# Attention with two MoE layers on one core: MoE 2 with its weight blocks outermost and converted in place, and 32x32 triangles inverted on 128 partitions

## The chip, the cores and the metric

One core of a Trainium2 chip runs the whole program. The metric is the device time of one execution, in microseconds (us); the kernel before takes 1393.04 us, the median of three runs (1391.51 to 1396.16).

## What is computed

A linear attention with a decaying state (4 batches, 8 heads, 768 steps, head size 40), then two feed-forward layers on its 3072 tokens of 320 values. MoE is the reference's own word for them; there is no routing.

```python
for t in range(S):
    y[:, :, t] = einsum('bhd,bhde->bhe', rt, state)
    Sa = einsum('bhde,bhe->bhd', state, at)
    state = state * wt[:, :, None, :] - einsum('bhd,bhe->bhde', Sa, bt) + einsum('bhd,bhe->bhde', vt, kt)
# moe 1: d_ff = 2048
h = x @ w_in
x = (h * clip(h + 3, 0, 6) / 6) @ w_out
# moe 2: d_ff = 1536
out = ((x @ w_a) * (x @ w_b)) @ w_out
```

All inputs but the five weight matrices are float32. The weights are float64, and the kernel turns their two 32-bit words into a float32 with one ScalarE and five VectorE instructions (`f32_steps`, L71 to L86). Every matmul of the two layers then runs on a high and a low float32r part (`split`, L128 to L130).

## The kernel before

The steps are cut into 12 chunks of 64 (`NCH`), each with 16 pairs of heads (`NP`) side by side. `window(j)` (L696) lists by hand the steps of chunk j together with those that prepare chunks j+1 and j+2; all five engines and the DMA queue of SP take their instructions in that order. Between these steps the table `MOE` puts in the steps of the first layer, 16 to a window from window 2 on, where a step is one `up` (16 matmuls) or one `down` (12 matmuls). One window is a period of the attention phase.

**The triangle.** Each chunk needs the inverse of unit triangular 64x64 matrices. Their two 32x32 diagonal blocks, 64 of them in all, go through DRAM (`t_load`, tensor `scr`) into `TA2` with one block to a partition. `t_solve` (L505 to L518) inverts them on POOL: 31 times a product (L515) and a subtraction (L518) over the part of the block that is left, on 64 partitions. Chunks take the lower and the upper 64 partitions in turn. `t_store` (L521 to L539), one window later, turns the result on ScalarE into `tnt` (L528, which uses the free rows of `TA2`), writes it both ways to DRAM (`n1`, `n2`, shown in the profile as `n`) and loads from there `NY` and `AB`; the first matmuls that read it are those of `merge_y` (L547).

**The weights of layer 2.** `WEIGHT` slots of the windows run `widen` (L744): in 68 pieces of 192 columns it loads float64 words (`ws`), converts them (`cv`), and stores float32 to DRAM (`w2af`, `w2bf`, `w2of`). A window has seven slots. After the last window come the 21 steps of layer 1 that are left, below called the tail of layer 1; beside them `moe2_weights` loads the float32 weights back and splits them, one piece after each step from the third on, in turn on POOL and VectorE.

**Layer 2.** `moe2`: for each of six groups of 512 tokens, for each of 12 blocks of 128 inner units, `up` (L842: 16 matmuls of 512 columns) and `down` (L864 to L866: 12 matmuls of 320 columns) into four accumulators that live through all 12 blocks; then the sums go to DRAM.

```python
ac.activation(out=g, in_=uf, func=AF.Relu, bias=bias3, scale=1.0)          # L313, in layer 1's up
g = wk1.tile([128, 512], F32, tag="g", name="g", bufs=1)
for f in window(j): ...   elif f == WEIGHT: next(wide2, None); next(wide2, None)
```

Of the kernel before, what the change touches and what calls it, by code (L numbers as in the profile page):

```python
# [23 lines left out]
NT = B * S  # L24
# [70 lines left out]
def attention_and_moe(ctx, tc, t, flag):  # L95
# [22 lines left out]
    w1 = m1.enter_context(tc.tile_pool(name="w1", bufs=1))  # L118
# [243 lines left out]
    TN2 = a1.tile([128, 32, 32], F32, name="TN2")  # L362
# [15 lines left out]
    def setup_first():  # L378
# [12 lines left out]
        gp.memset(TN2, 0.0)  # L391
# [5 lines left out]
        for z in n2:  # L397
            sp.dma_start(out=z.rearrange("a p s t -> (a p) s t")[:, :, 0:32], in_=TN2[0:32])

# [92 lines left out]
    def t_half(j):  # L492
        return slice(64 * (j % 2), 64 * (j % 2) + 64)

    def t_load(j, between=lambda: None):
# [8 lines left out]
        sp.dma_start(out=TA2[t_half(j)], in_=scr.rearrange("u a p s t -> (u a p) s t"))  # L504

    def t_solve(rws, eng):

        TA, TN, TT = TA2[rws], TN2[rws], TT2[rws]
        nr = rws.stop - rws.start
        eng.memset(TN, 0.0)  # L510
        eng.memset(TN.rearrange("q s t -> q (s t)")[:, 0:1024:33], 1.0)
        for u in range(31, 0, -1):
            n = 32 - u
            tv = TT[:, 0:u * n].rearrange("q (s t) -> q s t", s=u)
            eng.tensor_tensor(  # L515
                out=tv, in0=TA[:, 0:u, u:u + 1].to_broadcast([nr, u, n]),
                in1=TN[:, u:u + 1, u:32].to_broadcast([nr, u, n]), op=ALU.mult)
            eng.tensor_tensor(out=TN[:, 0:u, u:32], in0=TN[:, 0:u, u:32], in1=tv, op=ALU.subtract)  # L518

    def t_start(j):  # L520
        t_solve(t_half(j), gp)  # L521

    def t_store(j, between=lambda: None):
        TN = TN2[t_half(j)]
        r0 = t_half(j).start
        tnt = TA2[r0:r0 + 32]
        NY = py["NY"] = a2.tile([128, NP, 32], F32, tag="py", name="NY")
        ac.copy(out=tnt, in_=TN[0:32].rearrange("q s t -> q t s"))  # L528
        n1 = dram.tile([2, 2, NP, 32, 32], F32, tag="n1", name="n1", bufs=2)
        z, AB = n2[j % 2], ABs[j % 2]  # L530
        sp.dma_start(out=n1[0].rearrange("a p s t -> (a p) s t"), in_=TN[0:32])
        sp.dma_start(out=z.rearrange("a p s t -> (a p) s t")[:, :, 32:64], in_=TN[32:64])
        sp.dma_start(out=n1[1].rearrange("a p s t -> (a p) s t"), in_=tnt)
        between()
        for ab in range(2):
            r = 64 * ab
            sp.dma_start(out=NY[r:r + 32], in_=n1[1, ab].rearrange("p s t -> s p t"))
            sp.dma_start(out=AB[r + 32:r + 64], in_=z[ab].rearrange("p s t -> s p t"))
            sp.dma_start(out=AB[r:r + 32, :, 0:32], in_=n1[0, ab].rearrange("p s t -> s p t"))  # L539

    def merge_y(j):
        AB, NY = ABs[j % 2], py["NY"]
        ps = bank().rearrange("q (p c) -> q p c", p=NP)
        for p in range(NP):
            for ab in range(2):
                r = 64 * ab
                mm(ps[r + 32:r + 64, p], AB[r:r + 32, p, 32:64], NY[r:r + 32, p], start=True, stop=True)  # L547
# [192 lines left out]
    WC = (("w2a", 3 * FF2), ("w2b", 3 * FF2), ("w2o", 12 * DM))  # L740
    w2f = {n: (dram.tile([128, c], F32, name=n + "f") if wide else t[n].rearrange("q k c -> q (k c)")) for n, c in WC}

    def widen():
        pieces = [(t[n].rearrange("q k c -> q (k c)")[:, c0:c0 + 192], w2f[n][:, c0:c0 + 192])  # L744
                  for n, cols in WC for c0 in range(0, cols if wide else 0, 192)]
        loaded, made = [], None
        for i in range(len(pieces) + 3):
            if made:
                sp.dma_start(out=made[0], in_=made[1])
                made = None  # L750
            if i < len(pieces):
                loaded.append((pieces[i][1], words(pieces[i][0], sp)))
            yield
            if loaded and (i > 1 or i >= len(pieces)):
                dst, st = loaded.pop(0)
                made = dst, from_words(st)
            yield

    def moe2_weights(pool):
        r = {}  # L760
# [458 lines left out]
```

## Time and profile before

| | |
|---|---|
| median of 3 runs | 1393.04 us |
| the profiled execution | 1393.52 us |
| its span in the profile | 1391.7 us |
| setup and windows 0 and 1 | 0 to 253 us |
| windows 2 to 9 | 253 to 828 us, 69.7 to 73.2 us each |
| windows 10 and 11 | 828 to 888 and 888 to 926 us |
| tail of layer 1 | 926 to 978 us |
| layer 2 | 978 to 1392 us |
| TensorE / VectorE / ScalarE / GpSimd busy | 82% / 60% / 37% / 38% |

The windows are told apart by ScalarE's copy L528, which begins once in each. PE is TensorE's matmul, DVE is VectorE, ACT is ScalarE, POOL is GpSimd, SP the engine whose queue issues the DMAs. PEclk is TensorE's granted clock as a share of 2.4 GHz.

### The profile page before, as it was taken

The page shows a single profiled execution, that of the slowest core. Times are in us where ns is not written, and L with a number is a line of the kernel's source. Part 1 is how long each engine was busy: PE and PEld are TensorE (multiplying, and loading weights), DVE is VectorE, ACT ScalarE, POOL GpSimd, SP SyncE. Part 2 cuts the span into 40 slices and gives each one's busy share as a digit, 9 for nine tenths or more (in the row PEclk, how much of TensorE's full clock was granted, in tenths as well). Part 3 has the DMA queues.
Part 4 walks back from the last instruction along what each step waited for, and adds up shares of the span by engine and source line. Part 5 has one row for each costly group of instructions (what it writes and reads, how often), then busy time and mean ns, then how long its engine had stood idle before and what let it go on. Part 6 is the DMA issues. An engine that isn't in the chain of part 4 may idle for free.

```text
span 1391.7 us, 34838 instructions
## 1 busy us (share of the span) xinstructions
PE 1144.8 (82%) x14826; PEld 1039.0 (75%) x14826; DVE 837.0 (60%) x1297; ACT 520.8 (37%) x1071; POOL 526.3 (38%) x835
## 2 busy tenths in 40 slices
PE   1214439889798888888888889899999999999997
PEld 1214438878787787778878889799888888888886
DVE  7899777486867776777767776556532222222322
ACT  1243344445443444444344444345422222222221
POOL 4889008382818382747465656302200000000000
PEclk9998559989989899988898989899999999999999
DMA  6262451515142524242333333323410000000000
GB/s 175 50 161 68 108 137 30 138 53 141 58 115 68 130 72 119 74 125 76 106 96 107 95 92 80 97 74 105 128 28 20 24 19 23 20 23 20 2 18 22
DMA packets 139908, 107.82 MB, mean 77 GB/s; under 512 B 88448, under 2 KB 129024, under 8 KB 137728
## 3 DMA queue, kind: packets, MB, share of 16 engines
q1 hardware_dynamic: 139744, 105.51, 28.0%
q8 instruction: 118, 1.93, 0.6%
q14 instruction: 46, 0.38, 0.1%
HBM read 78.87 MB, written 26.61 MB: 76 GB/s over the span
## 4 chain that ended last, share of the span: by engine, by line
PE 39%; DVE 29%; DMA 11%; ACT 10%; issue 8%; SPq 2%; POOL 0%; DVEq 0%; ACTq 0%; POOLq 0%
PE att L842 19%; PE up L308 4%; PE ac L866 3%; PE ac L865 3%; PE ac L864 3%; DVE up L314 3%; DVE rw L448 3%; DVE cv L80 2%; DVE ws L84 2%; DMA n<-TA 2%; ACT sq L458 2%; ACT gh L129 2%; DVE ws L83 2%; DVE W L446 2%; ACT TA L528 2%
## 5 line engine op out<-in xcount | busy, mean ns | idle before, releaser
L515 POOL TENSOR_TENSOR TT<-TA,TN 64x31 f32<-64x31 f32 (+15 forms) x372 | 207.6, 558 | 323.9 <-DMA TA<-scr 295.5
L518 POOL TENSOR_TENSOR TN<-TN,TT 64x31 f32<-64x31 f32 (+15 forms) x372 | 220.1, 592 | 29.1
L848 DVE TENSOR_TENSOR g<-att,asb 128x512 f32<-128x512 f32 x72 | 49.8, 692 | 227.4 <-PE att L842 227.4
L328 PE MATMUL dn<-wo_h,gh 128*128 128x320 f32 x384 | 142.8, 372 | 14.7 <-ACT gh L129 14.6
L330 PE MATMUL dn<-wo_h,gl 128*128 128x320 f32 x384 | 135.1, 352 | 1.6 <-DVE gl L130 1.5
L329 PE MATMUL dn<-wo_l,gh 128*128 128x320 f32 x384 | 134.0, 349 | 0.0
L129 ACT CAST gh<-up 128x512 fp32r<-128x512 f32 x96 | 56.3, 586 | 185.4 <-DVE up L314 185.4
L308 PE MATMUL up<-xh,wi_h 128*128 128x256 f32 x384 | 108.2, 302 | 3.1 <-ACT xh L287 3.1
L130 DVE TENSOR_TENSOR gl<-up,gh 128x512 fp32r<-128x512 f32 x96 | 66.3, 691 | 62.6 <-ACT gh L129 62.6
L308 PE MATMUL up<-xh,wi_l 128*128 128x256 f32 x384 | 102.3, 288 | 0.0
L328 PEld LDWEIGHTS dn<-wo_h,gh 128*128 128x128 f32 x384 | 85.4, 222 | 20.6 <-ACT gh L129 16.1
L313 ACT ACTIVATE g<-up,bias 128x512 f32<-128x512 f32 x96 | 65.8, 686 | 91.8 <-PE up L308 90.7
L636 PE MATMUL att<-GH,KBT 128*64 128x64 f32 (+1 forms) x768 | 47.9, 285 | 62.0 <-DVE GH L615 60.7
L129 ACT CAST g2h<-g 128x512 fp32r<-128x512 f32 x72 | 44.7, 621 | 144.1 <-DVE g L848 144.1
L846 ACT COPY asb<-att 128x512 f32<-128x512 f32 x72 | 42.3, 587 | 147.6 <-PE att L842 147.6
L314 DVE SCALAR_TENSOR_TENSOR up<-g,up 128x512 f32<-128x512 f32 x96 | 66.0, 688 | 46.0 <-ACT g L313 46.0
L636 PEld LDWEIGHTS att<-GH,KBT 128*64 128x64 f32 (+1 forms) x768 | 39.7, 176 | 68.4 <-DVE GH L615 68.2
L864 PE MATMUL ac<-oh,g2h 128*128 128x320 f32 x288 | 88.8, 308 | 1.1 <-ACT g2h L129 1.1
L330 PEld LDWEIGHTS dn<-wo_h,gl 128*128 128x128 f32 x384 | 86.1, 224 | 4.6 <-DVE gl L130 4.6
L866 PE MATMUL ac<-oh,g2l 128*128 128x320 f32 x288 | 88.7, 308 | 0.2 <-DVE g2l L130 0.2
L865 PE MATMUL ac<-ol,g2h 128*128 128x320 f32 x288 | 88.8, 308 | 0.0
L448 DVE RECIPROCAL rw<-W 128x256 f32<-128x256 f32 x48 | 84.1, 1753 | 3.9 <-ACT sq L458 1.2
(170 smaller groups left out, 3050.8 us busy)
## 6 DMA issues: line engine op xcount, KB each, us to landing
RV<-in_rve_dram SPq DMA_DIRECT2D x24, 320.0 KB
KB<-in_kbe_dram SPq DMA_DIRECT2D x22, 320.0 KB
st<-in_w1i_dram SPq DMA_DIRECT2D x13, 384.0 KB
ws<-in_w2a_dram SPq DMA_DIRECT2D x24, 192.0 KB
ws<-in_w2b_dram SPq DMA_DIRECT2D x24, 192.0 KB
raw<-in_we_dram SPq DMA_DIRECT2D x24, 162.5 KB
LB<-in_ae_dram SPq DMA_DIRECT2D x24, 160.0 KB
VX<-in_vte_dram SPq DMA_DIRECT2D x24, 160.0 KB
```

The costliest lines, as they stand in the source:

```text
L129: ac.copy(out=hi, in_=src)
L308: mm(u[:, e], a_, b_, start=(n == 0), stop=(n == len(seq) - 1))
L328: mm(acc, gh[:, e, c0:c0 + 128], wo_h[:, m], start=(m == 0), stop=False)
L329: mm(acc, gh[:, e, c0:c0 + 128], wo_l[:, m], start=False, stop=False)
L330: mm(acc, gl[:, e, c0:c0 + 128], wo_h[:, m], start=False, stop=(m == 15))
L448: ve.reciprocal(out=rw, in_=w[:, :, 1:65])
L515: eng.tensor_tensor(out=tv, in0=TA[:, 0:u, u:u + 1].to_broadcast([nr, u, n]), in1=TN[:, u:u + 1, u:32].to_broadcast([nr, u, n]), op=ALU.mult)
L518: eng.tensor_tensor(out=TN[:, 0:u, u:32], in0=TN[:, 0:u, u:32], in1=tv, op=ALU.subtract)
L842: mm(u, a_, b_, start=(n == 0), stop=(n == len(seq) - 1))
L864: mm(acc, gh[:, sl], r["oh"][:, m], start=(m == 0), stop=False)
L865: mm(acc, gh[:, sl], r["ol"][:, m], start=False, stop=False)
L866: mm(acc, gl[:, sl], r["oh"][:, m], start=False, stop=(m == 11))
```

## The change

Three parts.

1. `widen`, its DRAM copies and its slots go. Layer 2 reads the float64 weights itself: class `Weights2` cuts each block m of 128 inner units into five pieces (256, 256, 256, 160 and 160 columns) and loads, converts and splits one piece at each call of `go`, two loads ahead, all on ScalarE and VectorE. The 15 pieces of blocks 0 to 2 are made in the tail of layer 1, the others inside layer 2, one after each `up` and `down`.
2. Layer 2 is turned round: four blocks of three inner units (`BLOCK`) outside, six groups of tokens inside. All six groups are transposed in the first block and stay in SBUF; the four accumulators are emptied after every block into `sum` tiles, with VectorE additions from the second block on.
3. The triangles are inverted on 128 partitions. Column t of the inverse goes to the lower or the upper half of the partitions by its parity, so that an instruction covers half the columns (2856 elements to a partition over the 31 products where there were 5456). `TA2` is loaded twice, `TL` is double, `tnt` is now a `wk1` tile with the tag `g`, and six stores take the place of three.

```diff
     def t_load(j, between=lambda: None):
...
-        sp.dma_start(out=TA2[t_half(j)], in_=scr.rearrange("u a p s t -> (u a p) s t"))
+        for h in range(2):
+            sp.dma_start(out=TA2[half(h)], in_=scr.rearrange("u a p s t -> (u a p) s t"))
...
     def t_start(j):
-        t_solve(t_half(j), gp)
+        TL = TLs[j % 2]
+        gp.memset(TL, 0.0)
...
+        for u in range(31):
+            m, n = 31 - u, u // 2 + 1
+            tv = TT2[:, 0:m * n].rearrange("q (t c) -> q t c", t=m)
+            gp.tensor_tensor(
+                out=tv, in0=TA2[:, u:u + 1, u + 1:32].rearrange("q a t -> q t a").to_broadcast([128, m, n]),
+                in1=TL[:, u:u + 1, 0:n].to_broadcast([128, m, n]), op=ALU.mult)
+            gp.tensor_tensor(out=TL[:, u + 1:32, 0:n], in0=TL[:, u + 1:32, 0:n], in1=tv, op=ALU.subtract)

     def t_store(j, between=lambda: None):
-        TN = TN2[t_half(j)]
-        r0 = t_half(j).start
-        tnt = TA2[r0:r0 + 32]
+        TL = TLs[j % 2]
+        tnt = wk1.tile([128, 16, 32], F32, tag="g", name="tnt", bufs=1)
...
-        sp.dma_start(out=n1[0].rearrange("a p s t -> (a p) s t"), in_=TN[0:32])
-        sp.dma_start(out=z.rearrange("a p s t -> (a p) s t")[:, :, 32:64], in_=TN[32:64])
-        sp.dma_start(out=n1[1].rearrange("a p s t -> (a p) s t"), in_=tnt)
+        ac.copy(out=tnt, in_=TL.rearrange("q t c -> q c t"))
+        for h in range(2):
+            r = 64 * h
+            sp.dma_start(out=n1[1].rearrange("a p t s -> (a p) t s")[:, :, 16 * h:16 * h + 16], in_=TL[r:r + 32])
+            sp.dma_start(out=n1[0].rearrange("a p (c h) t -> (a p) c h t", h=2)[:, :, h], in_=tnt[r:r + 32])
+            sp.dma_start(out=z.rearrange("a p (c h) t -> (a p) c h t", h=2)[:, :, h, 32:64], in_=tnt[r + 32:r + 64])
...
+        def go(self, last):
+            self.ahead()
...
+                w = to_f32(nc, st, cv[:, 0], cv[:, 1], st[:, :, 1])
...
+            if i < 2:
+                split(self.up[m][:, 4 * i:4 * i + 2], self.up[m][:, 4 * i + 2:4 * i + 4],
+                      w.rearrange("q (k c) -> q k c", k=2))
...
+            for tt in range(4):
+                acc, o = accs[g][tt][:, 0:DM], sums[g][:, tt]
+                if b:
+                    ve.tensor_tensor(out=o, in0=acc, in1=o, op=ALU.add)
...
+            for b in range(NM // BLOCK):
+                for g in range(NG):
+                    for i in range(BLOCK):
+                        m = BLOCK * b + i
...
+                        up(g, m)
+                        if b == 0 and g + 1 < NG and i:
+                            trans(2 * g + 1 + i)
+                        if prev:
+                            down(*prev)
+                        prev = (g, m)
+                        if g or i:
+                            w2.go(BLOCK * b + 2 * BLOCK - 1)
...
-                    elif j:
-                        next(wide2, None)
-                        next(wide2, None)
...
         while len(mq) > 2:
             moe_step()
             n += 1
             if n > WEIGHTS_2:
-                conv.go()
+                w2.go(BLOCK - 1)
```

ScalarE at the head of a window. `AB`, `KBT` and `NY` are copies of attention results out of PSUM, `g` is the Relu of layer 1. Before:

```order
L528 COPY TA_117<-TN_118 32x1024
L484 COPY AB_109<-att 64x512 x2
L313 ACTIVATE g<-up,bias_98 128x512
L129 CAST gh<-up 128x512
L484 COPY AB_109<-att 64x512 x2
L571 COPY KBT_111<-att 128x160 x4
L313 ACTIVATE g<-up,bias_98 128x512
```

and with the change:

```order
L528 COPY tnt<-TL_119 128x512
L485 COPY AB_109<-att 64x512 x2
L314 ACTIVATE g<-up,bias_98 128x512
L130 CAST gh<-up 128x512
L485 COPY AB_109<-att 64x512 x2
L572 COPY KBT_111<-att 128x160 x4
L314 ACTIVATE g<-up,bias_98 128x512
```

The order is the same, but `tnt` and `g` are now one buffer: the Relu behind the copy may write only when the four stores that read `tnt` have ended.

The queue of SP at the same place, from the stores of the inverse to the load of the next `KB` (`n_...` are the tensors `n1`, `n_1_...` the tensor `n2`). Before:

```order
L531 DMA n_5387<-TN_118 32x1024
L532 DMA n_1_121<-TN_118 1024x1x32
L533 DMA n_5387<-TA_117 32x1024
L537 DMA NY<-n_5387 32x16x32
L538 DMA AB_110<-n_1_121 32x16x64
...
L501 DMA scr<-AB_109 32x16x32 x4
L504 DMA TA_117<-scr 64x1024
L430 DMA KB<-in_kbe_dram 40x2048 x2
L749 DMA w2af<-cv_5246 128x192
L141 DMA ws<-in_w2b_dram 128x384
```

and with the change:

```order
L531 DMA n_5194<-TL_119 1024x1x16
L532 DMA n_5194<-tnt 512x1x32
L533 DMA n_1_122<-tnt 512x1x32
L531 DMA n_5194<-TL_119 1024x1x16
L532 DMA n_5194<-tnt 512x1x32
L533 DMA n_1_122<-tnt 512x1x32
L537 DMA NY<-n_5194 32x16x32
...
L501 DMA scr<-AB_109 32x16x32 x4
L505 DMA TA_117<-scr 64x1024 x2
L431 DMA KB<-in_kbe_dram 40x2048 x2
```

Runs of 4 KB (32x1024) and 128 bytes became runs of 64 bytes (1024x1x16) and 128 bytes (512x1x32); the load of `TA` is doubled; the stores and loads of `widen` are gone from behind `KB`.

VectorE in the tail of layer 1, between two `up` steps. Before:

```order
L314 SCALAR_TENSOR_TENSOR up<-g,up 128x512
L130 TENSOR_TENSOR gl<-up,gh 128x512
L130 TENSOR_TENSOR ol<-st,oh 128x320
L314 SCALAR_TENSOR_TENSOR up<-g,up 128x512
```

and with the change:

```order
L315 SCALAR_TENSOR_TENSOR up<-g,up 128x512
L131 TENSOR_TENSOR gl<-up,gh 128x512
L78 TENSOR_SCALAR ws_11827<-cv_11877 128x256
L80 SCALAR_TENSOR_TENSOR cv_11877<-cv_11877,ws_11827 128x256
L83 TENSOR_SCALAR ws_11827<-cv_11877 128x256
L84 SCALAR_TENSOR_TENSOR ws_11827<-ws_11827 128x256
L86 TENSOR_TENSOR cv_11877<-cv_11877,ws_11827 128x256
L135 TENSOR_TENSOR up_11824<-cv_11877,up_11824 64x256
```

(`up_11824` is the weight tile of one inner block, `up` without a number the PSUM tile of layer 1.) A second piece of six follows there before the next `up`: two conversions stand where one subtraction stood.

## Rows read from the trace of the kernel before

**Rows 1.** Stretches: length; busy us of PE, PEld, DVE, ACT, POOL; PEclk; DMA share; GB/s

```profile
470.50:542.80 72.30, 63.18 (x1094) 58.56 (x1090) 54.05 (x80) 31.52 (x67) 39.99 (x66) 0.91 0.36 95
542.80:614.60 71.80, 60.40 (x1060) 56.06 (x1061) 52.65 (x80) 31.68 (x69) 40.84 (x66) 0.88 0.38 104
...
828.10:888.30 60.20, 55.40 (x1052) 52.53 (x1042) 39.01 (x68) 28.63 (x58) 33.59 (x62) 0.94 0.35 90
...
926.00:978.00 52.00, 51.08 (x430) 49.62 (x428) 31.97 (x51) 24.24 (x46) 9.31 (x9) 1.00 0.35 109
```

**Rows 2.** Waits of PE in windows 2 to 9: us in total, times, longest

```profile
PE att L636 <- DVE GH L615: 42.6, 24, 3.1
PE dn L328 <- ACT gh L129: 13.1, 6, 3.3
```

**Rows 3.** The stretch of 4 us behind one such wait

```profile
514.00:518.00 4.00, 3.62 (x37) 3.27 (x38) 3.86 (x8) 1.20 (x3) 3.53 (x7) 0.50 0.00 0
```

**Rows 4.** Timeline of DVE in one window: start us, us, instruction

```profile
485.60 0.20 DVE L78 TENSOR_SCALAR ws<-cv 128x192 int32<-128x192 int32 x1
...
486.91 0.36 DVE L86 TENSOR_TENSOR cv<-cv,ws 128x192 f32<-128x192 f32 x1
...
504.91 0.70 DVE L78 TENSOR_SCALAR ws<-cv 128x192 int32<-128x192 int32 x1
...
513.53 1.28 DVE L615 TENSOR_TENSOR GH<-att,mask 128x512 f32<-128x512 f32 x2
```

**Rows 5.** Groups by line: the five VectorE instructions of one conversion

```profile
L78 DVE TENSOR_SCALAR ws<-cv 128x192 int32<-128x192 int32 (+1 forms) x75 | 28.0, 374 | 8.6 <-ACT cv L77 8.6
L80 DVE SCALAR_TENSOR_TENSOR cv<-cv,ws 128x192 int32<-128x192 int32 (+1 forms) x75 | 49.0, 654 | 2.6
L83 DVE TENSOR_SCALAR ws<-cv 128x192 int32<-128x192 int32 (+1 forms) x75 | 32.6, 435 | 2.6
L84 DVE SCALAR_TENSOR_TENSOR ws<-ws 128x192 f32<-128x192 uint32 (+1 forms) x75 | 45.4, 606 | 2.6
L86 DVE TENSOR_TENSOR cv<-cv,ws 128x192 f32<-128x192 f32 (+1 forms) x75 | 41.2, 549 | 2.6
```

**Rows 6.** Timeline of DVE in that window, where it waits for KB

```profile
492.66 1.01 DVE L464 TENSOR_TENSOR KB<-KB,rw 128x512 f32<-128x512 f32 x1 [3.66 <-DMA KB<-in_kbe_dram]
```

**Rows 7.** Timeline of SP's queue at the head of that window: start, issue time, DMA

```profile
472.55 0.33 SPq L533 DMA_DIRECT2D n<-TA  x1
477.68 0.32 SPq L537 DMA_DIRECT2D NY<-n  x1
...
480.71 2.09 SPq L501 DMA_DIRECT2D scr<-AB  x4
...
485.14 0.84 SPq L430 DMA_DIRECT2D KB<-in_kbe_dram  x2
```

**Rows 8.** The chain that ended last, in layer 2: two ups in a row

```profile
1100.73 3.73 PE att L842 x16
1106.23 3.74 PE att L842 x16
```

**Rows 9.** Groups by line: the inversion on POOL

```profile
L518 POOL TENSOR_TENSOR TN<-TN,TT 64x31 f32<-64x31 f32 (+15 forms) x372 | 220.1, 592 | 29.1
L515 POOL TENSOR_TENSOR TT<-TA,TN 64x31 f32<-64x31 f32 (+15 forms) x372 | 207.6, 558 | 323.9 <-DMA TA<-scr 295.5
```

**Rows 10.** Timeline of DVE in the tail of layer 1: the second and the last up

```profile
938.74 0.70 DVE L314 SCALAR_TENSOR_TENSOR up<-g,up 128x512 f32<-128x512 f32 x1 [1.48 <-ACT g L313]
...
975.30 0.69 DVE L130 TENSOR_TENSOR gl<-up,gh 128x512 fp32r<-128x512 f32 x1 [0.65 <-ACT gh L129]
```

**Rows 11.** Groups by line: a split in ScalarE and VectorE, and a sum from PSUM

```profile
L260 ACT CAST wo_h<-cv 128x192 fp32r<-128x192 f32 (+1 forms) x4 | 1.3, 324 | 11.6 <-DVE cv L86 11.6
L262 DVE TENSOR_TENSOR wo_l<-cv,wo_h 128x192 fp32r<-128x192 f32 (+1 forms) x4 | 1.3, 325 | 1.6 <-ACT wo_h L260 1.6
L654 DVE TENSOR_TENSOR ST<-att,ST 104x320 f32<-104x320 f32 x22 | 10.5, 479 | 1.2 <-PE att L652 1.2
```

More of the change, by code (lines that the diff above doesn't have):

```diff
@@ L361, in attention_and_moe @@
     TA2 = a1.tile([128, 32, 32], F32, name="TA2")
-    TN2 = a1.tile([128, 32, 32], F32, name="TN2")
+    TLs = [a1.tile([128, 32, 16], F32, name=f"TL{i}") for i in range(2)]
     TT2 = a1.tile([128, 256], F32, name="TT2")
@@ L736, in window @@
         return out
[L740 to L757, printed above, removed]
@@ L861, in down @@
                 sl = slice(128 * tt, 128 * tt + 128)
[L862 to L879 removed]
+                mm(acc, gh[:, sl], w[:, 0], start=(i == 0), stop=False)
@@ new lines, in down, with total @@
+                mm(acc, gh[:, sl], w[:, 1], start=False, stop=False)
+                mm(acc, gl[:, sl], w[:, 0], start=False, stop=(i == BLOCK - 1))
+            if i == BLOCK - 1:
+                total(g, b)
+        def total(g, b):
+            if b == 0:
+                sums[g] = (xr if g < 4 else left()).tile([128, 4, DM], F32, name=f"sum{g}")
+            for tt in range(4):
+                acc, o = accs[g][tt][:, 0:DM], sums[g][:, tt]
+                if b:
+                    ve.tensor_tensor(out=o, in0=acc, in1=o, op=ALU.add)
+                elif tt % 2:
+                    ac.copy(out=o, in_=acc)
+                else:
+                    ve.tensor_copy(out=o, in_=acc)
+                if (b + 1) * BLOCK == NM:
+                    r0 = 512 * g + 128 * tt
+                    sp.dma_start(out=t["out"][r0:r0 + 128, :], in_=o)
@@ L881, in rest @@
         def rest():
-            load_x(1)
             prev = None
-            for g in range(NG):
-                for m in range(12):
-                    up(g, m)
-                    if g == 0:
-                        conv.go(3)
-                    if prev and (g, m) != (NG - 1, 11):
-                        down(*prev)
-                        prev = None
-                    prev = prev + (m,) if prev else (g, m)
-                    if m == 8 and g + 1 < NG:
-                        trans(g + 1)
-                        if g + 2 < NG:
-                            load_x(g + 2)
+            load_x(2)
@@ new lines, in rest @@
+            for b in range(NM // BLOCK):
+                for g in range(NG):
+                    for i in range(BLOCK):
+                        m = BLOCK * b + i
+                        if b == 0 and g + 1 < NG:
+                            h = 2 * g + 2 + i
+                            if i < 2:
+                                load_x(h + 1) if h + 1 < 2 * NG else None
+                        up(g, m)
[6 more added lines that the diff above has]
+                            w2.go(BLOCK * b + 2 * BLOCK - 1)
@@ L958, in moe_step @@
                 mq.pop(0)()
-        wide2 = widen()
         for j in range(NCH):
```

225 lines of the change are left out of this document (108 added, 117 removed).

## The prediction

> **What bounds the kernel now.** I read the busy time by stretch first, then the waits of TensorE in the windows, then the timelines of VectorE and SP inside one window, and last the tail of layer 1 and the chain in layer 2.
>
> In a window of the attention phase TensorE is busy 60 to 63 of 72 us [rows 1]. The 9 us of idle time are not all of the loss: the granted clock means 0.91 and 0.88 over these windows, so another 6 to 8 us go in matmuls at the lower of the two clocks, 1.2 GHz. Both together make 15.6 us (9.1 + 0.09 x 72.3) in the first row and 20 us in the second. Work at 2.4 GHz is thus some 52 to 57 us, and no window can fall below that.
>
> The longest wait of TensorE is that of L636 for the mask product `GH` on VectorE, 42.6 us in eight windows, 5.3 us each [rows 2]. Behind it the clock is at 1.2 GHz: PEclk 0.50 in the 4 us after one such wait, with TensorE busy [rows 3]. The second wait is that of a `down` for `gh` (13.1 us), in every other window, where VectorE stands before the load of `KB`.
>
> Why is `GH` late? The reader sees it on VectorE. One conversion of `widen` stands right ahead: it begins at 504.91, and `GH` ends at 514.8 [rows 4]. A conversion on a quiet chip takes 1.67 us (485.60 to 487.27); its five instructions mean 0.374 + 0.654 + 0.435 + 0.606 + 0.549 = 2.62 us [rows 5], since most stand beside POOL's inversion, and the one at 504.91 took 3.8. Seven in a window make 18 of the 53 us that VectorE is busy [rows 1].
>
> VectorE is also held by DMA: 3.66 us until `KB` has landed, at 492.66 [rows 6]. That load is the last link of a chain on SP's queue at the head of the window: stores of the inverse (last one issued at 472.55), their landing, loads of `NY` (477.68), stores of `scr` (480.71), loads of `TA` and `KB` (485.14) [rows 7].
>
> In layer 2 nothing but TensorE counts: two ups begin 5.50 us apart [rows 8], and 72 of these make 396 of its 414 us. The tail of layer 1 is TensorE's too: 51 of 52 us [rows 1].
>
> **The change, part by part.** *Windows 2 to 9: `widen` goes.* In the window of rows 5 the conversion before `GH` costs 3.8 us, and TensorE waits up to 3.1 us there [rows 2]; more of them stand between the first and the second `GH`. With VectorE's 18 us away both `GH` waits end, 5.3 us a window, and with them some two thirds of the clock loss of 7.5 us (mean of the rows), 5 us. Gain 10.3 us, if nothing else comes late.
>
> *What is late next.* `KB` does not land sooner: behind its landing stand 18.4 us of VectorE work up to `GH`'s end (514.8 - 492.66 - 3.75), so `GH` can't end before 41 us into the window (it began at 470.5), and TensorE, which waited up to 3.1 us, was there at about 41 as well. The doubled `TA` load lies ahead of `KB` in the queue: 0.5 us of issue and 256 KB more, about 1 us if the 896 KB of `TA` and `KB` land within 7.5 us of 485.14 now, part of it fixed; against that the stores of `widen` are gone from the bulk loads ahead. I take `KB` 1.5 us later; bounds 0 and 4.
>
> *The Relu behind `tnt`.* The copy L528 is halved (512 elements for 1024: 1 us less). But the Relu of the next `up` now waits until the stores that read `tnt` have landed. Before, the last store was issued 2.1 us after the window began and `NY` could be loaded at 7.2 [rows 7]. Now six stores are issued; I take 8 us. What stands behind the Relu on ScalarE: the copies of `AB` that free two PSUM banks, then `KBT`. TensorE has a `down` and an `up` to go on with, 3.7 us together by the pace of the tail (37.25 us for ten ups, below), then lacks a bank for L568: 2 to 3 us of waiting that were not there, partly in the time in which it waited for `NY` before. I charge 2.3 us with the clock. Sum for a window: -10.3 + 2.3 = -8, bounds -3 (`KB` 4 us later, so that `GH` gains little) and -12 (the Relu's wait falls into `NY`'s). Eight windows: -64 us (-24 to -96).
>
> *Windows 10 and 11.* Window 10 loses 4.8 us idle and 3.6 by the clock, all behind one `GH` with conversions ahead: -6 (-3 to -8). Window 11 starts with five layer-1 steps behind `tnt`: +1 (-1 to +4).
>
> *The inversion.* 62 instructions mean 0.59 and 0.56 us, 35.6 us a chunk [rows 9]. Half the elements make that 18 us if all of it goes with elements, 36 if none does; I take 25. It isn't on the path either way: it begins when `TA` has landed, some 17 us into a window (the load behind it is issued at 14.6), and is asked for at the next one's start, over 60. What it buys is VectorE's peace: in the setup VectorE works beside two inversions, so -4 us there (-10 to +4, since squares of the setup share `tnt`'s buffer too).
>
> *The tail of layer 1.* From the second `up`'s product, 938.74, to the last `up`'s `gl`, 975.99, it takes 37.25 us [rows 10]. Now 15 conversions stand there in line on VectorE and ScalarE, each in turn waiting for the other. One of 256 columns: 1.67 us scaled by columns with a fixed part, 2.0, then the high part on ScalarE and the low one on VectorE, 0.32 each at 192 columns [rows 11], 0.8 with 0.1 of hand-over: 2.9 us; one of 160 columns 2.15. Nine and six make 39. Ten ups at 2.4 (Relu done to `gl`: 0.70, 0.65 for the cast, 0.69 [rows 10], and hand-overs) make 24, other VectorE work 2: 65 us, 28 more than before, and TensorE waits. Layer 2 then begins with a second load of `x` that has to wait for the first's transposes, and with TensorE at 1.2 GHz: +4. Together +32; bounds +11 (VectorE's time alone, 48 us) and +40 (loads late by 0.5 us each).
>
> *Layer 2.* TensorE's work is the same. Beside each 5.50 us stand 2.05 us of product, cast and `gl`, 2.6 us of conversion, and a share of four sums per block and group, 0.48 each [rows 11], 0.65: 5.3 us in line. It is covered, by 0.2 us. +4 (0 to +15).
>
> Sum: -64 - 6 + 1 - 4 + 32 + 4 = -37 against the profiled execution's 1393.5 us, which is the median of the runs (1393.0) but for 0.5: **1356 us**; with its own range 1325 to 1385 (the bounds, not all at one end).
>
> A rule of the Trainium skill speaks against this change. The rows show stores of 128-byte runs (`scr`, 4 x 512 of them) issued by 482.8 and landed before the loads behind them were issued, by 485.14 [rows 7], so in about 2 us. The skill's page "DMA: Bandwidth & Descriptors" (Specifications) says that below 512 bytes the engines read, modify and write, and so miss the full rate. By the row the six stores are paced by their issue, as I have it; and the sum stays 1356; by the page stores of 64 bytes would land later, towards the first rival's 1432, and no row here shows how much.
>
> **The rivals.** *The stores of `tnt` become the pace (slower).* `tnt` and `g` are one buffer, and 4096 runs of 64 and 128 bytes go out where 1088 did (64 of them of 4 KB). Should they land at 12 us instead of 8, the Relu, `AB`, `NY`, `scr` and `KB` all come 4 us later, TensorE waits 7 us in the head of the window and is at 1.2 GHz for 4 us more: a window keeps its 72 us. Then 0 + 3 for the windows, 0 for the setup, +32 + 4: 1432 us. It decides from 11 us on, where a window gains under 4. For it: nothing in the trace shows a store of 64-byte runs, and all of the queue is in line behind it. Against: 128-byte runs pass quickly. 0.16.
>
> *`KB` is the pace (no change).* `KB` lands 4 us later, `GH` with it: 4 us a window, -32 - 5 - 4 + 34 + 5: 1391 us. For it: VectorE's 18.4 us behind `KB` reach 41 us already. Against: after `GH` nothing of this holds. 0.17.
>
> *VectorE was all of it (much faster).* The Relu's wait hides in `NY`'s, shorter blocks on POOL quicken VectorE too, and a window falls to 60, 12 less: -96 - 8 - 7 + 20 + 2: 1304 us. For it: window 10, without `KB`, already runs at 60 with conversions. 0.15.
>
> That the change doesn't do what it says is excluded by the order of the instructions.
>
> **The numbers.** My forecast has 0.52. The range leaves out most of the slow rival and half of the fast one: 1312 to 1404 us. Within 0.3% (4 us, about what a measurement of this kernel tells from no change) lies a part of the `KB` case only. Faster: 0.52 + 0.15 + 0.07 of the `KB` case; the same 0.06; slower 0.20.
>
> **What would show it.** Right: windows of 64 us, no `GH` among TensorE's waits, a new wait of ScalarE's L314 for the stores of `tnt` of some 5 us a window, the tail of layer 1 about 30 us longer with VectorE over 70% busy there, ups 5.5 us apart in layer 2. Wrong: windows over 68 us (stores or `KB`), a tail without that growth, or ups further apart than 5.6 us.

## The result, and the profile after

The changed kernel takes **1326.66 us** (median of 4 runs, 1322.13 to 1329.49) where the kernel before, run beside it on the same chip, takes 1392.28 (1386.87 to 1396.16): a ratio of 0.953 with a 95% interval of 0.948 to 0.957. The forecast was 1356 us with a range of 1312 to 1404. The profiled execution has a span of 1323.0 us, 68.7 us less than the 1391.7 of before. Cut at the same events, the two traces differ like this (us; a window starts with the copy into `tnt`):

| stretch | before | after | difference | forecast |
|---|---|---|---|---|
| setup, windows 0 and 1 | 253.1 | 246.1 | -7.0 | -4 |
| windows 2 to 9 | 574.9 | 490.2 | -84.7 | -64 |
| window 10 | 60.3 | 58.2 | -2.1 | -6 |
| window 11 to the second `up`'s product | 50.5 | 49.5 | -0.9 | +1 |
| tail of layer 1, to the last `gl` | 37.2 | 64.7 | +27.4 | +28 |
| rest: into layer 2, layer 2 | 415.7 | 414.3 | -1.4 | +4 and +4 |

First the stretches of after: two windows, the tail, the first part of layer 2 (length; busy us of PE, of PEld, which is TensorE's loading of weights, of DVE, ACT and POOL; PEclk; DMA share; GB/s).

```profile
494.20:555.20 61.00, 57.58 (x1088) 54.52 (x1081) 34.04 (x45) 28.32 (x62) 29.70 (x67) 0.92 0.36 87
555.20:616.90 61.70, 57.38 (x1088) 54.32 (x1083) 34.08 (x45) 28.32 (x62) 29.60 (x67) 0.92 0.35 85
844.01:908.68 64.67, 43.63 (x267) 39.98 (x265) 45.98 (x116) 22.80 (x52) 0.00 (x0) 0.89 0.23 68
911.50:1000.00 88.50, 86.74 (x458) 74.17 (x458) 58.74 (x136) 34.62 (x81) 0.00 (x0) 1.00 0.27 79
```

A window is 61 us where it was 72 [rows 1]: VectorE is busy 34 us instead of 53, and TensorE stands idle 3.4 to 4.3 us instead of 9 to 11. In the tail TensorE is busy 44 of 65 us, and was 51 of 52; VectorE is at 71% there. Layer 2 is TensorE's, as before.

Next what PE waits for in windows 2 to 9 (us in total, times, longest).

```profile
PE att L569 <- ACT KBT L572: 31.8, 8, 6.5
PE att L482 <- issue: 1.4, 1, 1.4
PE dn L329 <- ACT gh L130: 0.8, 1, 0.8
```

The 42.6 us behind `GH` are gone and the 13.1 behind `gh` all but gone [rows 2], and so are two smaller waits of before:

```profile
PE att L547 <- DMA NY<-n: 9.6, 8, 2.1
PE att L568 <- DVE LB L488: 7.1, 6, 1.9
```

One wait is new, 4 us a window at the transposes of `KB`. Its source stands among the waits of ACT over the same windows:

```profile
ACT g L314 <- DMA n<-tnt: 55.1, 8, 9.2
```

and it shows again among those of DVE:

```profile
DVE up L315 <- ACT g L314: 101.7, 40, 9.1
...
DVE KB L465 <- DMA KB<-in_kbe_dram: 18.3, 8, 4.0
```

The Relu waits 6.9 us a window for the stores of `tnt`, and the copies of `KBT` stand behind it on ScalarE. SP's queue shows the head of the window that begins at 494.20 (start, issue time, DMA):

```profile
496.63 2.58 SPq L531 DMA_DIRECT2D n<-TL  x1
...
499.96 0.63 SPq L533 DMA_DIRECT2D n<-tnt  x1
501.73 0.33 SPq L537 DMA_DIRECT2D NY<-n  x1
...
505.60 2.09 SPq L501 DMA_DIRECT2D scr<-AB  x4
509.48 1.13 SPq L505 DMA_DIRECT2D TA<-scr  x2
510.70 0.84 SPq L431 DMA_DIRECT2D KB<-in_kbe_dram  x2
```

And on DVE, with the idle time ahead of an instruction in brackets:

```profile
517.90 0.69 DVE L465 TENSOR_TENSOR KB<-KB,rw 128x512 f32<-128x512 f32 x1 [1.46 <-DMA KB<-in_kbe_dram]
...
535.04 1.28 DVE L616 TENSOR_TENSOR GH<-att,mask 128x512 f32<-128x512 f32 x2
```

`KB` is issued 16.5 us into the window and multiplied at 23.7, where it was 14.6 and 22.2 [rows 6, 7]. Over windows 2 to 9 the means are 17.3 and 24.7, and 15.8 and 23.2 before. `GH` now begins 40.8 us into the window and no longer at 43.0 [rows 4]; TensorE does not wait for it. The inversion is shorter: the groups of the page give 393 and 421 ns as the mean of an instruction, so that 62 of them make 25.2 us a chunk, where those of [rows 9] make 35.6.

```profile
L517 POOL TENSOR_TENSOR TT<-TA,TL 128x126 f32<-128x126 f32 (+22 forms) x372 | 146.3, 393 | 340.1 <-DMA TA<-scr 311.8
...
L520 POOL TENSOR_TENSOR TL<-TL,TT 128x126 f32<-128x126 f32 (+22 forms) x372 | 156.8, 421 | 29.1
```

In the tail, the timeline of DVE shows the second `up`'s product, one conversion of 256 columns, and the last `gl`. The first and the last line are the same events as in [rows 10].

```profile
844.01 0.69 DVE L315 SCALAR_TENSOR_TENSOR up<-g,up 128x512 f32<-128x512 f32 x1 [1.48 <-ACT g L314]
...
850.64 0.29 DVE L78 TENSOR_SCALAR ws<-cv 128x256 int32<-128x256 int32 x1
...
852.22 0.43 DVE L86 TENSOR_TENSOR cv<-cv,ws 128x256 f32<-128x256 f32 x1
853.11 0.42 DVE L131 TENSOR_TENSOR up<-cv,up 128x256 fp32r<-128x256 f32 x1 [0.47 <-ACT up L130]
...
907.99 0.69 DVE L131 TENSOR_TENSOR gl<-up,gh 128x512 fp32r<-128x512 f32 x1 [0.65 <-ACT gh L130]
```

The next conversion begins at 853.46, so one takes 2.82 us. In layer 2, the chain of waits shows ups 5.49 and 5.50 us apart, as in [rows 8]:

```profile
1095.79 3.73 PE att L847 x16
...
1101.28 3.74 PE att L847 x16
...
1106.78 3.73 PE att L847 x16
```

### The profile page after: what moved, and what is told of

It reads as the page before. It is cut to its first block, busy times and chain, and to the rows that moved or that the text cites. A ratio compares the mean times of both kernels' runs of the same rounds, so it can differ in the third digit from the quotient of the medians.

```text
span 1323.0 us, 34883 instructions
## 1 busy us (share of the span) xinstructions
PE 1110.3 (84%) x14826; PEld 1013.2 (77%) x14826; DVE 771.6 (58%) x1371; ACT 504.5 (38%) x1087; POOL 375.0 (28%) x829
## 4 chain that ended last, share of the span: by engine, by line
PE 63%; DVE 9%; ACT 9%; DMA 7%; POOL 5%; issue 4%; SPq 4%; ACTq 0%; DVEq 0%; POOLq 0%
PE att L847 20%; PE up L309 10%; PE dn L329 4%; PE dn L331 3%; PE dn L330 3%; PE ac L871 3%; PE ac L870 3%; PE ac L869 3%; POOL TL L520 2%; POOL TT L517 2%; DMA n<-tnt 2%; PE att L614 2%; PE att L637 2%; PE att L631 2%; PE att L588 2%
## 5 line engine op out<-in xcount | busy, mean ns | idle before, releaser
L517 POOL TENSOR_TENSOR TT<-TA,TL 128x126 f32<-128x126 f32 (+22 forms) x372 | 146.3, 393 | 340.1 <-DMA TA<-scr 311.8
L847 PE MATMUL att<-x2h,up 128*128 128x512 f32 x720 | 237.2, 394 | 0.2 <-ACT x2h L831 0.2
L847 PE MATMUL att<-x2l,up 128*128 128x512 f32 x432 | 170.4, 394 | 1.9 <-DVE x2l L832 1.9
L520 POOL TENSOR_TENSOR TL<-TL,TT 128x126 f32<-128x126 f32 (+22 forms) x372 | 156.8, 421 | 29.1
L847 PEld LDWEIGHTS att<-x2h,up 128*128 128x128 f32 x720 | 135.0, 188 | 29.2 <-ACT x2h L831 0.5
L331 PE MATMUL dn<-wo_h,gl 128*128 128x320 f32 x384 | 128.9, 336 | 1.4 <-DVE gl L131 1.4
L852 DVE TENSOR_TENSOR att<-att,asb 128x512 f32<-128x512 f32 x72 | 50.4, 700 | 97.9 <-PE att L847 79.3
L130 ACT CAST gh<-up 128x512 fp32r<-128x512 f32 x96 | 56.3, 586 | 114.8 <-DVE up L315 110.8
L847 PEld LDWEIGHTS att<-x2l,up 128*128 128x128 f32 x432 | 81.0, 188 | 19.4 <-DVE x2l L832 3.5
L869 PE MATMUL ac<-dn,g2h 128*128 128x320 f32 x288 | 89.5, 311 | 0.0
L871 PE MATMUL ac<-dn,g2l 128*128 128x320 f32 x288 | 88.6, 308 | 0.1
L870 PE MATMUL ac<-dn,g2h 128*128 128x320 f32 x288 | 88.7, 308 | 0.0
```

Source lines behind the costliest of these rows:

```text
L331: mm(acc, gl[:, e, c0:c0 + 128], wo_h[:, m], start=False, stop=(m == 15))
L517: gp.tensor_tensor(out=tv, in0=TA2[:, u:u + 1, u + 1:32].rearrange("q a t -> q t a").to_broadcast([128, m, n]), in1=TL[:, u:u + 1, 0:n].to ...
L520: gp.tensor_tensor(out=TL[:, u + 1:32, 0:n], in0=TL[:, u + 1:32, 0:n], in1=tv, op=ALU.subtract)
L847: mm(u, a_, b_, start=(n == 0), stop=(n == len(seq) - 1))
L869: mm(acc, gh[:, sl], w[:, 0], start=(i == 0), stop=False)
L870: mm(acc, gh[:, sl], w[:, 1], start=False, stop=False)
```

## The experiments

The theory: the windows gained because the conversions left VectorE, and the new inversion costs them the Relu's wait. Rivals: the shorter inversion brought part of the gain; the wait costs nothing, since another stands behind it; `KB` is what sets the window. Each version was timed beside the kernel before on the same chip; its ratio to that is given with the 95% interval. Lengths of windows are from the traces, one of each version. The kernel before took 1392 to 1401 us (medians) on the chips used, so that a difference of some 4 us between the windows of two versions (0.6% of 575) can be one between chips.

### The two halves of the change apart

*The old inversion in the changed kernel.* `t_load`, `t_start`, `t_store` and `merge_y` are those of before; layer 2 and the windows without `widen` are those of after:

```diff
-    TLs = [a1.tile([128, 32, 16], F32, name=f"TL{i}") for i in range(2)]
+    TN2 = a1.tile([128, 32, 32], F32, name="TN2")
...
     def t_start(j):
...
+        t_solve(t_half(j), gp)
```

> After with the old inversion (62 instructions on 64 partitions, its own tnt, three stores), the layer-2 change kept. Theory (VectorE's freedom from conversions brought all of the windows' gain): windows of 57 to 61 us, no wait of the Relu; the setup gives back 4 to 7 us; 1300 to 1325 us. Rival (the shorter inversion on POOL brought a good part of the gain, since VectorE is slower beside it): windows of 65 us and more, 1355 to 1380.

Measured: 1317.07 us, ratio 0.940 (0.936 to 0.944). Windows 2 to 9 take 479.8 us, 60.0 each: 95.1 us less than before and 10.4 less than after; the setup with windows 0 and 1 takes 251.8 us, 5.7 longer than after. The theory holds: the removal of `widen` brings the whole gain of the windows, and there the new inversion takes back 1.3 us a window. TensorE's longest wait in windows 2 to 9 is here one for POOL:

```profile
PE att L482 <- POOL LB L454: 26.5, 14, 2.6
```

It stands idle for 31.2 us in them, against 34.6 after, and is busy 448.6 us at a mean granted clock of 0.95, against 455.6 at 0.93. So about a third of the 10.4 us is waiting, and the rest goes with the clock.

*The new inversion in the kernel before.* The same four functions exchanged the other way; `widen` and the old layer 2 stay.

> Before with the new inversion alone; widen and the old layer 2 stay. Theory (the inversion by itself buys nothing in a window and brings the Relu's wait): windows within -1 and +4 us of the 71.9 of before, the GH wait still near 5 us a window, setup 4 to 7 us shorter; 1377 to 1420 us. Rival (the inversion is part of the gain): windows 3 us or more shorter, 1355 to 1368.

Measured: 1394.66 us, ratio 0.995 (0.992 to 0.998); windows 575.5 us, where before has 574.9. The setup did not get its 4 to 7 us (254.0 against 253.1), so what the inversion gives there shows only together with the rest of the change, and the traces do not say why. The waits of PE in this version's windows 2 to 9:

```profile
PE att L634 <- DVE GH L613: 42.8, 24, 5.0
PE att L566 <- ACT KBT L569: 37.9, 8, 5.3
```

The wait for `GH` stayed, and the one for `KBT`, 37.9 us, took the place of those for `gh`, `NY` and `LB`, 29.8 us. Yet VectorE did profit from the shorter inversion: it is busy 389.4 us in these windows for the same 640 instructions, and was 423.8. So 4.3 us of VectorE a window came free, and the windows are no shorter. That the new wait of the Relu used up what VectorE gained is inferred; no run separates the two.

### The conversions' arithmetic, or their transfers?

The kernel before, with `widen`'s loads, stores and slots. Of a conversion only ScalarE's first step is left, and the five VectorE instructions are left out, so layer 2 gets wrong weights:

```diff
-                made = dst, from_words(st)
+                made = dst, wk1.tile([128, 192], F32, tag="cv", name="cv2", bufs=2)[:, 0:st.shape[1]]
+                ac.activation(out=made[1], in_=st[:, :, 1].bitcast(F32), func=AF.Copy, scale=2.0 ** -112)
```

> Before, with widen's loads and stores as they are, but of each conversion only ScalarE's first step between them, nothing on VectorE (so layer 2 computes with wrong weights). Theory (the conversions' time on VectorE is what the windows lost): windows of 59 to 63 us, no GH wait, 1295 to 1320 us. Rival (widen's bulk transfers in queue and memory cost it): windows of 68 us and more, 1360 to 1392.

Measured: 1303.83 us, ratio 0.935 (0.929 to 0.942); windows 2 to 9 take 493.6 us. PE's longest waits in them:

```profile
PE att L481 <- POOL LB L453: 21.8, 13, 1.9
PE dn L328 <- ACT gh L129: 6.3, 6, 2.8
```

There is no wait for `GH`. This version, before, and the changed kernel with the old inversion all invert in the old way, so their differences split the gain of the windows: VectorE's five instructions are worth 81.3 us (574.9 to 493.6), and the transfers with ScalarE's step 13.8 (493.6 to 479.8).

### The head of a window: the Relu's wait and KB's place

*`tnt` in the half of `TA`'s buffer that is free at that time.*

```diff
-        tnt = wk1.tile([128, 16, 32], F32, tag="g", name="tnt", bufs=1)
+        tnt = TA2[:, 0:16] if j else wk1.tile([128, 16, 32], F32, tag="g", name="tnt", bufs=1)
```

> After, with tnt of chunks 1 to 11 in the lower half of TA's buffer in place of the Relu's g (TA is loaded again only 15 us into the window, when the stores have landed). Theory (the Relu's wait is what the new inversion costs in a window): the wait of L314 for n<-tnt falls from 65.4 us to under 10, TensorE's wait for KBT from 31.8 us to under 10, a window is at least as short as the 60.0 us of the old inversion, against 61.3, and the setup stays that of after: 1300 to 1316 us. Rival (the wait only stands in front of the next one: the loads of NY and AB, then KB, set the pace): TensorE waits at L547 for NY or at L637 for GH instead, windows of 61 us, 1319 to 1328.

Measured: 1323.21 us, ratio 0.948 (0.941 to 0.955), which can't be told from after. The Relu's wait is gone, and the windows take 493.4 us, not less than the 490.2 of after. The waits of PE in windows 2 to 9:

```profile
PE dn L329 <- ACT gh L130: 18.0, 7, 3.9
PE att L547 <- DMA NY<-n: 15.4, 11, 3.2
```

One wait of DVE there:

```profile
DVE KB L465 <- DMA KB<-in_kbe_dram: 50.9, 8, 7.9
```

The theory falls here. VectorE, no longer held by a late Relu, comes to `KB` sooner and waits 6.4 us a window for it instead of 2.3, since `KB` is issued no earlier (17.3 us into a window on average, as in after); `gh`, queued behind, is late for TensorE. The rival held: the Relu's wait stood in front of those for `NY` and for `gh`, 33.4 us together, where it had cost 31.8.

*`KB` ahead of `TA`, and `tnt` in `TA`'s buffer.* In windows 1 to 9 SP issues the load of `KB` before the two loads of `TA`, which first have to wait for `scr` to land. The inversion is issued behind them:

```diff
+    def kb_ta(j):
+        load_kb(j + 2)
+        t_ta(j + 1)
+        t_start(j + 1)
...
-            + on(ahead, (op_kbt, j + 1, 2), (op_kbt, j + 1, 3)) + on(nx2 and j, (load_kb, j + 2))
+            + on(ahead, (op_kbt, j + 1, 2), (op_kbt, j + 1, 3)) + on(nx2 and j, (kb_ta, j))
```

> The version with tnt in TA's buffer, and in windows 1 to 9 the load of KB goes ahead of TA's loads on SP's queue, as soon as the transposes of the old KB are issued; TA's loads and the inversion come behind it. Theory (with six stores and two TA loads the queue of SP sets when KB lands, and that sets the window): KB's load is issued 3 us sooner after the window's start than the 16.4 us of the version with TA first, VectorE's wait for KB falls from 50.9 us in the eight windows to 15 to 30, windows of 58.5 to 60 us against 61.7, 1302 to 1314 us. Rival (the loads of NY and AB behind the stores are the pace, and KB is hidden behind the merges): VectorE's wait falls, but the windows stay at 61 to 62 us, 1317 to 1326.

Measured: **1294.70 us**, ratio 0.928 (0.922 to 0.935); windows 464.0 us, 58.0 each, better than expected. SP's queue, in the window that begins at 481.4:

```profile
494.24 0.75 SPq L431 DMA_DIRECT2D KB<-in_kbe_dram  x2
496.90 1.12 SPq L513 DMA_DIRECT2D TA<-scr  x2
```

DVE's wait for `KB` over windows 2 to 9, where the version with `TA` first has 50.9 us:

```profile
DVE KB L465 <- DMA KB<-in_kbe_dram: 14.1, 7, 3.3
```

PE's longest wait there:

```profile
PE att L560 <- DMA NY<-n: 19.3, 12, 4.0
```

`KB` is issued 12.9 us into the window shown, not 16.5 (means of the eight: 14.2 and 17.3). TensorE is left with 2.4 us a window behind `NY`; the mean granted clock over these windows is 0.97, in after 0.93, in before 0.89.

*`KB` ahead of `TA`, `tnt` with the Relu as in after.* The edit before, without that of `tnt`.

> KB ahead of TA, but tnt in the Relu's buffer again, as after has it. Theory (with KB's wait gone nothing covers the Relu's any more): the Relu waits 6 to 7 us a window, TensorE 4 of them at the transposes of KB, with the clock the prediction's 2.3 us a window or more: windows of 60 to 63 us against 58.0, 1311 to 1330. Rival (NY's loads come as late as the Relu's wait ends, so that it is covered by them): windows within 0.8 us of 58.0, 1293 to 1301.

Measured: 1321.38 us, ratio 0.946 (0.940 to 0.952); windows 483.2 us, 60.4 each. PE's longest wait in them:

```profile
PE att L582 <- ACT KBT L585: 27.3, 8, 5.1
```

So the Relu's wait costs nothing that shows while `KB` is late, and 2.4 us a window (483.2 to 464.0) once it is not; `KB`'s place is worth 0.9 us a window while the Relu waits (490.2 to 483.2), 7.0 us in eight, not far above what chips differ by, and 3.7 once it does not (493.4 to 464.0). By the medians either edit alone gives after less than 1% (1326.66 to 1323.21 and to 1321.38), and both give 2.4%.

*`KB` ahead of `TA`, with the old inversion.* The edit before, with the old inversion, its own `tnt` and its three stores.

> KB ahead of TA and the old inversion, its own tnt and three stores. Theory (the queue of SP, with three stores and a TA load more, was the whole price of the new inversion in a window, 10.4 us in eight; with KB ahead that price falls away, and the 36 us of the old one, begun some 17 us into a window of 58, end close to the next window's start and hold POOL's product for LB and VectorE beside it): windows of 58 to 61 us and a setup 4 to 6 us longer, 1298 to 1320. Rival (fewer stores stay worth 1.3 us a window): windows of 56 to 57.5, 1284 to 1294.

Measured: 1347.13 us, ratio 0.965 (0.960 to 0.971), slower than either side expected: windows 505.7 us, 63.2 each, where the old inversion behind `TA` first took 60.0. PE's one large wait in windows 2 to 9:

```profile
PE att L482 <- POOL LB L454: 50.3, 15, 5.9
```

And the timeline of POOL, its product for `LB` in two windows that follow each other:

```profile
506.72 4.40 POOL L454 TENSOR_TENSOR LB<-LB,W 64x1024 f32<-64x1024 f32 x2
...
570.31 4.39 POOL L454 TENSOR_TENSOR LB<-LB,W 64x1024 f32<-64x1024 f32 x2
```

The product stands behind the inversion on POOL and begins only with the next window (506.8); `op_a`, `AB`, `scr`, `TA` and the next inversion hang on it. POOL stands idle in these windows only until `TA` has landed. That is a loop through POOL, and 63.6 us is its period. The edit made it longer: `TA` is issued 17.4 us into a window on average, and was at 15.8 with `TA` first, where TensorE already waited 26.5 us for this product. `KB` came no sooner, at 16.3 us in both. Here lies what the new inversion is good for: with `KB` ahead it is worth 41.7 us in these windows (505.7 to 464.0), after a cost of 10.4 without.

### The tail of layer 1

*Conversions in three parts.* ScalarE's first step is issued a piece earlier, the cast and the subtraction a piece later:

```diff
         def go(self, last):
             self.ahead()
+            self.finish()
...
+            self.pend = m, i, cv[:, 1].bitcast(F32)
+            if self.loaded and self.loaded[0][0] <= last:
+                self.begin(self.loaded[0][2])
```

> After, with each conversion of layer 2's weights cut in three: ScalarE's first step is issued one piece earlier, and the cast to the high part with the subtraction one piece later, so that neither engine stands for the other inside a piece. Theory (the tail of layer 1 is bound by VectorE and ScalarE waiting for each other in turn): VectorE's waits for the casts of weights go (15 of 0.39 to 0.47 us) and so do ScalarE's 33 us behind cv; the tail falls from 64.7 us to 51 to 57 us, 1313 to 1320 us in all. Rival (the loads of the pieces, each behind its buffer's last reader, set the pace of the tail): ScalarE's first step waits for the loads instead, tail 62 us or more, 1323 to 1328.

Measured: 1326.16 us, ratio 0.951 (0.945 to 0.958); tail 64.8 us, no gain. Of ScalarE's waits in it, three are new (ACT, us in total, times, longest):

```profile
ACT ws L77 <- DMA ws<-in_w2b_dram: 7.3, 3, 2.7
...
ACT ws L77 <- DMA ws<-in_w2o_dram: 6.2, 5, 1.9
...
ACT ws L77 <- DMA ws<-in_w2a_dram: 4.1, 2, 2.6
```

The first step, asked for earlier, finds its load not landed: 17.6 us. The rival held for this version. It does not show that loads bound the tail of after, where this wait does not occur.

*The subtraction on POOL besides*, `ve` to `gp` in these splits.

> The same, and the subtraction of the conversions on POOL, which has nothing else to do there. Theory (VectorE's time is the bound then): 15 x 0.33 to 0.43 us less on VectorE, tail of 45 to 52 us, 1306 to 1316 us. Rival (beside POOL VectorE gets slower, as it did in the windows of before): the conversion's five instructions on VectorE take 20% more or longer, no gain over the version with the subtraction on VectorE.

Measured: 1325.58 us, ratio 0.951 (0.944 to 0.958); tail 63.4 us. ScalarE's wait for the loads is still there, so the tail cannot show what VectorE's time is worth. But the rival is seen: the subtraction takes 5.8 us off VectorE (15 times 0.33 to 0.43), and the five instructions that stay take 30.0 us for the 15 conversions and not 25.5. Beside POOL VectorE lost most of what it gave away.

*A third staging buffer besides*, `bufs=3` for `ws2` and three loads ahead.

> The version with conversions in three parts and the subtraction on POOL, with three staging buffers for the pieces instead of two. Theory (with the first step issued a piece earlier, two buffers made the load late; what bound the tail before was VectorE and ScalarE in turn): the waits of ScalarE's first step for its load, 17 us, fall under 6, the tail falls from 64.8 us to 48 to 57, 1309 to 1319 us. Rival (a load can't follow faster, 3.5 us from issue to use whatever the buffers): tail 62 us or more, 1322 to 1328.

Measured: 1314.90 us, ratio 0.944 (0.937 to 0.951); tail 55.1 us, and no wait for a load in it. So both theories had half of it: the turns of VectorE and ScalarE do bind the tail, and taking them apart is worth 9.5 us against after, but only with a buffer more, since a first step a piece earlier needs its load a piece earlier. The third buffer without the parts was not run; in after it would find no wait for a load to end. The stretch of the tail in this version:

```profile
841.75:896.88 55.13, 41.25 (x267) 37.80 (x265) 43.87 (x101) 22.07 (x52) 9.83 (x15) 0.94 0.29 82
```

VectorE is busy 80% of it, and was 71% in after. What bounds the rest was not tried.

*Five of the fifteen conversions moved into layer 2.*

```diff
+                        if b == g == 0 and i < 2:
+                            w2.go(BLOCK - 1)
+                            w2.go(BLOCK - 1)
...
-                w2.go(BLOCK - 1)
+                w2.go(BLOCK - 2)
```

> After, with only ten of the fifteen conversions in the tail, and the five of unit 2 in the first two ups of layer 2, two a step. Theory (each conversion in the tail costs its whole chain, 2.3 to 2.9 us, while TensorE stands idle a third of the time; an up of layer 2 covers one and not two): tail 64.7 - 13 = 52 us, layer 2 longer by 4 to 7 us, 1316 to 1321 us. Rival (the conversions cost the same wherever they stand, being VectorE's time): 1325 to 1330.

Measured: 1324.10 us, ratio 0.949 (0.942 to 0.956), no gain, and just under the rival's stretch. The tail fell to 56.3 us, 8.4 less, and the rest rose from 414.3 to 423.3. The longest of PE's waits in layer 2 is then this one, for a conversion:

```profile
PE att L847 <- DVE up L135: 3.0, 1, 3.0
```

A conversion moved there costs 1.8 us (9.0 / 5), and cost 1.7 in the tail (8.4 / 5). The rival held: it costs the same in either place.

### Both gains together

The version with `KB` ahead and `tnt` in `TA`'s buffer, with the tail of the three staging buffers.

> KB ahead of TA and tnt in TA's buffer, with the conversions of the tail in three parts, the subtraction on POOL and three staging buffers. Theory (the two gains lie in different stages and add): 1294.7 less the 10 us that the tail gained (1314.9 against 1325.6): 1280 to 1288 us, windows of 58 us, tail of 55. Rival (the gains overlap, what the windows save is waited for in the tail): 1291 to 1298.

Measured: **1288.67 us** (1283.61 to 1289.07), ratio 0.922 (0.917 to 0.928); windows 463.8 us, tail 55.2. By the traces both stages have their gain at once, so the two add, and the time is 0.7 us above the expected stretch. By the medians the tail brought 6.0 us on top of the windows (1294.70 to 1288.67) where some 10 were expected. This is the fastest version: a ratio of 0.922 to before, where after has 0.953.

## Why the prediction was right, and where it was off

Step by step, with the prediction's own terms.

**`widen` goes: right for VectorE, in both parts.** The `GH` waits were to end, 5.3 us a window, and with them 5 us of the clock: 82.4 us in eight windows. The version with the copies alone, which takes nothing but VectorE's five instructions away, has no `GH` wait and gains 81.3 us. Its TensorE stands idle some 5.5 us a window less and is busy some 4.5 us a window less, which is the clock (0.893 to 0.945). In the whole change the idle time fell from 83.5 to 34.6 us (574.91 - 491.39 and 490.21 - 455.60), and the busy time for the same 8592 matmuls by 35.8 us (0.89 to 0.93). Two readings behind the term were loose and changed nothing in it: the conversion said to stand right ahead of `GH` ends 4.9 us before it, with seven other instructions of VectorE between, and the wait for `gh` came in six of the eight windows, not in every other one.

**`widen`'s transfers: a term that was missing.** The sum had nothing for its loads and stores beyond their effect on `KB`. They and ScalarE's step were worth 13.8 us of the windows. No run separates the two.

**"The Relu behind `tnt`", +2.3 us a window: right as a wait, far too dear as a cost.** The wait came as described: the Relu begins 8.3 us into the window shown and 9.1 on average (taken: 8), and TensorE waits 4 us for a bank at the transposes (taken: 2 to 3). But I added it to a sum that counted nothing else, and it is not additive. In the kernel before, the new inversion brought 37.9 us of this wait in eight windows, took away 29.8 for `gh`, `NY` and `LB`, and cost 0.6 us. In the changed kernel it cost 10.4, not 18.4, with everything else that it brings. The text did say "partly in the time in which it waited for `NY`", and did not work that part out. The 2 x 2 of the runs is plainer still: with `KB` late, removing the wait gains nothing; with `KB` early it is worth 2.4 us a window, nearly the figure charged.

So the 20.7 us by which the windows beat the forecast are 13.8 for the transfers and 8.0 for the inversion, less 1.1 for VectorE. The parts are taken in this order; as the 0.6 shows, another order divides them otherwise.

**"`KB` 1.5 us later": right.** It is multiplied 24.7 us into a window on average and was at 23.2. `GH` begins at 40.8 in the window shown; 41 us was the bound given for its end. That the window now hangs on `KB` was named as a rival at no change; it holds in a weaker form: with the new inversion the windows stayed at 61 us and more while `KB` stood behind `TA`, and came to 58 with `KB` ahead and the Relu's wait gone.

**The rivals.** The stores of `tnt` did not become the pace: the Relu could go on 7.7 to 11.4 us into a window, 9.1 on average, not at 12. "VectorE was all of it", 1304 us, came nearest in the windows (-96 forecast there, -84.7 measured), but charged 20 us to the tail, where 27 came.

**The inversion: off in both directions.** 25 us a chunk as taken. "It isn't on the path either way" holds for the new one in after, and is wrong for the old one in a shorter window: in windows of 60 us TensorE waits 26.5 us for POOL's product behind it, and with `KB` ahead it closes a loop of 63 us. The price of the new one, 10.4 us in the windows, had no term but the Relu's and `KB`'s; how it divides between the six stores, the second load of `TA` and the shared buffer was not tried one by one.

**The tail: right.** 65 us forecast, 64.7 measured; a conversion of 256 columns 2.82 us (2.9), one of 160 columns 2.30 (2.15, from 881.95 to 884.25). Its cause, turns of two engines, held, with the buffers as a second lock that only the runs showed.

**Layer 2: too dear by 9.4 us, the largest miss outside the windows.** Ups are 5.5 us apart as forecast and the sums are covered; of +4 and +4 nothing is seen, but -1.4. The wait for the second load of `x` is there (3.5 us), but the first `up` begins 3.2 us after the last `gl`, and did so 1.8 us after it before: 1.4 us more. From the last `up` to the program's end it is 10.3 us, and was 12.7.

**Setup and window 10** were -7.0 and -2.1 against -4 and -6: the errors nearly cancel, which is luck.

## What to carry to other kernels

When a new wait is forecast at the head of a stage, list every wait that the stage already has, further on and on other engines too. Such waits do not add: time lost at the head is time that the later ones no longer need, and the gain of removing one shows only when the next is gone as well. So try such edits in pairs; here two that gave under 1% each alone gave 2.4% together. And when work is issued one step earlier, count the buffers that its loads land in first: a step issued a piece sooner needs a load issued a piece sooner.

## What the runs showed of the hardware

- VectorE slowed beside POOL in some instructions and not in others. In windows 2 to 9 the five instructions of 56 conversions took 157.9 us of VectorE in before and 126.6 with the new inversion alone, same shapes. The other 360 instructions there took the same in sum under either inversion: 271.4 us (after, POOL busy 237) and 271.7 (old inversion, POOL busy 316). Two parts of that sum differ and cancel: `KB<-KB,rw` means 769 ns in after and 896 with the old inversion, `ST<-ST,W` 716 and 492, and both have their inputs in SBUF. With an input in PSUM, `GH<-att,mask` means 684 ns in both, and `up<-g,up` 689 and 691. The Trainium skill's "SBUF — State Buffer" (section "SBUF: two separate sides") says that VectorE and GpSimd take one port pair as an exclusive lock, so that the loser waits out the other's instruction; VectorE takes it in a two-port mode or, against a GpSimd instruction that reads SBUF, with two inputs in SBUF. The conversions work from SBUF to SBUF, and the trace agrees in direction.
- Stores in short runs moved slowly. The first of these stretches holds loads issued ahead of them, mostly in runs of 8 KB, the second the second store of `TL` (64 KB in runs of 64 bytes), the third the two stores behind it (128 bytes):

```profile
492.00:493.50 1.50, 1.50 (x11) 1.50 (x12) 0.00 (x0) 1.48 (x3) 0.00 (x0) 1.00 0.76 217
500.00:500.50 0.50, 0.50 (x5) 0.50 (x4) 0.00 (x0) 0.00 (x0) 0.00 (x0) 1.00 0.84 89
501.25:501.75 0.50, 0.50 (x7) 0.50 (x6) 0.00 (x0) 0.00 (x0) 0.00 (x0) 1.00 0.78 126
```

The DMA engines were busy 76%, 84% and 78% of these stretches and moved 217, 89 and 126 GB/s. At this size the loss is little: in this window the last of the six issues ended at 500.59, the load of `NY`, which waits for the stores of `TL`, was issued at 501.73, and the Relu, which waits for those of `tnt`, began at 502.49. The Trainium skill's "DMA: Bandwidth & Descriptors" (Specifications) says that transfers below 512 bytes miss the full rate. The trace agrees in the rate, and the stores still did not take the 12 us of the rival.
- The issue of the second store of `TL` takes 2.58 us in the window shown and 0.9 to 3.7 in the eight, that of most others 0.6. It does so too where `tnt` has its place in `TA`'s buffer (2.17 us in the same window). While it lasts, from 496.63 to 499.21, the DMA engines are 89% busy. No run here tells why it is long.
- The granted clock rose as TensorE's idle time fell: the same 8592 matmuls were busy 491 us at a mean granted clock of 0.89, 456 at 0.93 and 442 at 0.97, with 83.5, 34.6 and 22.1 us of idle time. The sum of the idle time alone does not set it: with `tnt` in `TA`'s buffer it was 0.945 at 38.2 us.
